# Four short attention runs for the first two head groups, and VectorE in ScalarE's place in the preparation of token blocks

## The chip, the cores and the metric

The kernel runs on one core of a Trainium2 chip. The metric is the device time of one execution, in microseconds. Four compute engines matter: TensorE (PE) multiplies matrices, ScalarE (ACT) evaluates functions such as the exponential, VectorE (DVE) and GpSimd (POOL) do elementwise work, and SyncE (SP) issues most of the transfers. Each runs its own instructions strictly in order and waits for the others by semaphores.

## The reference

One transformer block with adaptive layer norm, on 2048 tokens of width 512 and 32 heads of width 16:

```python
x = A_x
mod = (_silu(c) @ w_mod).reshape(c.shape[0], 6, 1, -1)
sa, ca, ga, sb, cb, gb = (mod[:, 0], ..., mod[:, 5])
h = _layernorm(x) * (1 + ca) + sa
x = x + ga * _A_ref(h, A_wqkv, A_wo)      # softmax(q k^T / 4) v, 32 heads, then wo
h = _layernorm(x) * (1 + cb) + sb
x = x + gb * _B_ref(h, B_w1, B_b1, B_w2, B_b2)   # w1 (512 x 1376), gelu, w2
```

## The kernel before

**Tiles and runs.** Tokens are cut into four blocks of 512 (`b` = 0 to 3) and sixteen key tiles of 128 (`kt`). The heads are cut into four column groups of eight (`cc`), each into two halves of four heads (`par`). One *run* is the attention of four heads for one block of 512 queries over a list of key tiles; the four heads of a run share the rows of TensorE. A *unit* is the score tile of one head and one key tile, 128 keys by 512 queries. A run over all sixteen tiles has 64 units, and the whole kernel has 2048 units' worth of scores.

**Who takes the exponential.** Most units go to ScalarE: TensorE writes three or two units into a PSUM tile `st` (`qk_a`, matmuls recorded at `qk`'s lines 940 and 944), and one ACTIVATE at line 998 turns them into `pt`. The two sizes alternate, 128x1536 and 128x1024, with one `st` tile each and four `pt` buffers each. The tiles in `shared` (key tiles 2, 5, 8, 11 and 14, `DKS`) go to VectorE where it gets to them first: it adds a constant to the scores (line 1052, `ph`), so that the integer, read as bf16, approximates the exponential, and makes shifted copies (`ph` at line 1087, `sh` at line 1096, and GpSimd pieces at line 1103), which are multiplied by v and by a weighted v (`VWB`). The products with v are accumulated in one PSUM tile `od` (line 1147), which VectorE copies out when a run ends (`normalise`, line 1214). Denominators then go through transfers on SP's queue (`dn`, `dc`, `rn`, `RB`), and GpSimd multiplies by the reciprocals.

**The start.** Before k, q and v of a token block exist, its 512 tokens have to be loaded, normalised (VectorE: line 660 and 661 statistics, line 676 normalisation, with the root on GpSimd, line 671), transposed by TensorE, modulated by (1 + ca) and sa into `blk` (`modulate`, line 686 on ScalarE or line 689 on VectorE), multiplied by the weights (`make_k`, `make_v`, `make_q`), and cast from PSUM to `kT` (line 694 on ScalarE or line 696 on VectorE) and to `VEB` (line 696). To begin early, the first two runs (`SUB = 2`: the two halves of group 0 for query block 0) read only key tiles 0 to 3, that is the first token block, and leave their partial sums in SBUF (`kept`). Runs 2 and 3 are the same two halves over key tiles 4 to 15, and `normalise` adds the kept sums (line 1211). From run 4 on all sixteen tiles are read. Blocks 1 and 2 (`PARTS`) are modulated and cast in two parts of 256 tokens, the first part's modulations on VectorE and the second part's on ScalarE; blocks 0 and 3 in whole rows. In this text the second and third token blocks are `b` = 1 and 2 in the code.

**The order.** The kernel writes its own instruction order. A planner (`Plan`) in the program keeps a list of ready operations for each engine, with assumed durations, and issues the one with the best priority (`dyn`); VectorE's units of a run may begin only when ScalarE has reached that run (`d_job` and the main loop's test against `a_run`). A small pseudo-random term (`spread`) is added to the priorities, seeded by one entry of `SEEDS` for each 12.5 us of planned time. So the table `SEEDS` picks one order out of many. Nothing is decided at run time.

Of the kernel before, what the change touches and what calls it, by code (L numbers as in the profile page):

```python
# [11 lines left out]
ACT = mybir.ActivationFunctionType  # L12
# [43 lines left out]
AL = 0.06  # L56
FILL = 1.6
SPREAD = 0.3
SEEDS = (47, 74, 926, 0, 261, 311, 918, 742, 253, 869, 717, 310, 0, 77, 989, 722, 609, 0, 307, 361, 371, 367, 117, 577, 633, 569, 261, 103, 97, 26, 695, 543, 331, 469, 527, 375, 85, 71, 0, 418, 210, 266, 573, 349, 750, 566, 887, 0, 37, 0, 351, 423, 527, 370, 279, 111, 267, 2, 850, 0, 0, 0, 0, 0, 0, 0)
HEAT = 1.45  # L60
RISK = 0.2

# [207 lines left out]
def kernel(  # L270
# [19 lines left out]
    NC = D // P  # L290
    NT = S // P
    QB = 512
    NQ = S // QB
    LAST = NQ - 1
    TPB = QB // P
# [49 lines left out]
    PARTS = (1, 2)  # L345
# [269 lines left out]
    def silu(o):  # L615
# [8 lines left out]
              prio=0.0, rel=(o_tr,))  # L624
# [167 lines left out]
    def make_k(b, cc, kind, acq, eng, after=None):  # L792
        if b in PARTS and cc == 0:
            o_k[(cc, b)] = []
            for part in range(2):
                cols = slice(2 * part * P, 2 * (part + 1) * P)
                mm = chain([(lambda ps, j=j, cols=cols: nc.tensor.matmul(
                    out=ps[:, 0:2 * P], lhsT=o_w[1].tile[:, j, 0:P], rhs=o_h[b].tile[:, j, cols],
                    start=(j == 0), stop=(j == NC - 1)), MM / 2) for j in range(NC)], [o_w[1], o_w0[1]], kind, acq,
                    (o_h[b], o_w[1]), need=lambda j, part=part: o_hd[b][NC * part + j])  # L800
                o_k[(cc, b)].append(op(eng, lambda o, mm=mm, cols=cols: copy(eng, kT[cc][b][:, cols], mm.tile[:, 0:2 * P]),
                                       0.33, (mm,), prio=0.3, rel=(mm,)))
            return
        if b == cc == 0:
            turns, mm, o_k[(cc, b)] = (0, 2, 1, 3), None, []
            for e, lo in (("ACT", 0), ("DVE", 2 * P)):
                cols = slice(lo, lo + 2 * P)
                mm = chain([(lambda ps, n=n, j=j, cols=cols: nc.tensor.matmul(
                    out=ps[:, 0:2 * P], lhsT=o_w[1].tile[:, j, 0:P], rhs=o_h[0].tile[:, j, cols],
                    start=(n == 0), stop=(n == NC - 1)), MM / 2) for n, j in enumerate(turns)], [o_w[1], o_w0[1], mm], kind, acq,  # L810
                    (o_h[0], o_w[1]), need=lambda n: o_hd[0][turns[n]])
                o_k[(cc, b)].append(op(e, lambda o, e=e, mm=mm, cols=cols: copy(e, kT[0][0][:, cols], mm.tile[:, 0:2 * P]),
                                       0.27 if e == "ACT" else 0.33, (mm,), prio=0.01 if e == "ACT" else 0.2, rel=(mm,)))
            return
        mm = proj(b, o_w[1], cc, kind, acq, after)
        o_k[(cc, b)] = op(eng, lambda o: copy(eng, kT[cc][b], mm.tile[:, 0:QB]), 0.6 if eng == 'DVE' else 0.5, (mm,), prio=0.3,
                          rel=(mm,))
# [54 lines left out]

    early = [(1, 0),(0, 1),(1, 1)]
    groups = [(0, 0)] + early + [(b, cc) for b in range(NQ) for cc in range(NC) if (b, cc) not in [(0, 0)] + early]
    SUB = 2
    runs = [(0, p) for p in range(SUB)] + [(b, 2 * cc + p) for b, cc in groups[:LAST * NC] for p in range(2)] + [(LAST, u) for u in range(6)] + [(LAST, 6), (LAST, 7)] * 2
    wait = {cc: 2 * groups.index((0, cc)) for cc in range(NC)}
    NR = len(runs)
    HB = QB // 2
# [8 lines left out]


    def tiles_of(r):  # L890
        return range(len(PAIRS)) if r in part_of else range(TPB) if r < SUB else range(TPB if r < 2 * SUB else 0, NT)
    shared = [[0, 1] if r in part_of else [kt for kt in (() if r < SUB else FIRST_DKS if r == SUB else DKS)
                                           if kt in tiles_of(r)] for r in range(NR)]
    own = [[kt for kt in tiles_of(r) if kt not in shared[r]] for r in range(NR)]
# [52 lines left out]
                         qm.tile[rows, :, hb * HB:(hb + 1) * HB], start=True, stop=True)  # L947

    def qk_deps(r, kt):
        n = r if r < SUB else r - SUB  # L950
        want_q(n // 2 + 1 + (n >= LAST * 8 - 4) if n < LAST * 8 - 2 else n - LAST * 4 + 3)
        cc, par, hb = run_heads(r)
        qm, evs = o_q[(cc, runs[r][0])]
        got = [evs[par or 0]]
        for t in key_tiles(r, kt):
            k = o_k[(cc, t // TPB)]
            got.append(k[t % TPB // 2] if isinstance(k, list) else k)
        return got, qm
# [243 lines left out]
        o_mv[n] = dma(shift, (ml,), kb=32, n=5.4, prio=0.5)  # L1202
    o_mv = [None, None]

    kept = []

    def normalise(r):
        last, od = o_last[r], o_od[r]
        if r in range(SUB, 2 * SUB):
            OD = kept[r - SUB]  # L1210
            got = op("DVE", lambda o: nc.vector.tensor_tensor(out=OD.tile, in0=od.tile, in1=OD.tile, op=ALU.add), 0.6,
                     (last, OD), lat=0.3, prio=0.0, rel=(od,))
        else:
            got = OD = op("DVE", lambda o: nc.vector.tensor_copy(out=o.tile, in_=od.tile), 0.6, (last,), lat=0.3,  # L1214
                          prio=0.0, acq=r_OD, rel=(od,))
        if r < SUB:
            kept.append(OD)
            return
        st = {}

        def d1(o):
            st["dn"] = drp.tile([4, QB], FP32, name="dn")
            nc.sync.dma_start(out=st["dn"], in_=OD.tile[16:P:32, :])
        o1 = dma(d1, (got,), kb=8, n=1.4, prio=0.0)
        o2 = dma(lambda o: nc.sync.dma_start(
            out=o.tile, in_=st["dn"].rearrange("i (s e) -> (i s) e", e=16)), (o1,), kb=8, n=1.4, prio=0.0,
            acq=r_dc)
# [24 lines left out]
        def shift(o):  # L1252
            for i in range(4):
                nc.sync.dma_start(out=to.tile[32 * i + 16:32 * i + 32, 0:HB] if b == LAST else
                                  to.tile[32 * i + 16:32 * i + 32, :],
                                  in_=OT.tile[32 * i:32 * i + 16, HB:QB] if b == LAST else
                                  OT.tile[32 * i:32 * i + 16, :])
        mv = dma(shift, two + ([] if b == LAST else to.two), kb=64, n=5.4, prio=0.5,
                 rel=() if b == LAST else (OT,))
        to.two = [mv]  # L1260
        if b == LAST:
            o_OT[(b, u)] = OT
# [326 lines left out]
    for b in range(NQ):  # L1589
        kind = f"in{b}"  # L1590
        urgent.add(kind)
        o_h[b], o_hd[b], za, trs = layer_norm(
            lambda t, b=b: o_x[b].tile[:, t, :], o_x0 if b == 0 else [o_x[b]] * TPB, modA, o_mA, prev_tr, r_blk,
            ("DVE", "ACT") if b in PARTS else ("DVE", "DVE", "ACT", "ACT") if b < 3 else ("DVE",) * 4, tuple(r_st[::-1]) if b == 0 else (r_ax, r_ax), kind, 0.6 + 0.2 * b, after, by_part=b in PARTS)
        prev_tr = trs[-1]
        if b == 0:
            op("NIL", first_done, 0.0, za, lat=0.0, prio=0.0)
        o_h[b].uses += 1
        free(o_x[b], za)
        if b == 0:  # L1600
            make_q(0, 0, kind, None)
        after = [za[-1]] * TPB if b else [o_hd[0][2]] * 1 + [o_q[(0, 0)][1][0]] * 3
        make_k(b, 0, kind, r_ax, "ACT")
        make_v(b, 0, kind, r_ax, "DVE", None if b else o_k[(0, 0)][0])
    o_w[0].uses += 1
    for cc in range(1, NC):
# [26 lines left out]
    while True:  # L1633
# [7 lines left out]
        while ended:  # L1641
            r = ended.pop(0)
# [90 lines left out]
```

## Time and profile before

| | us |
|---|---|
| median of 3 runs | 752.58 |
| lowest, highest | 752.27, 754.48 |
| the profiled execution | 752.77 |
| its span in the trace | 751.0 |
| granted TensorE clock, share of full speed | 0.997 |

The span runs from the first to the last instruction; the execution's own time has some 1.8 us around it. In a list of groups each row gives the line, the engine, the operation, output and inputs with partitions x elements, and the count; behind the bar come the busy time in us and the mean duration in ns, and behind the second bar the time the engine sat idle in front of these instructions and what ended it. In a timeline each row gives the start in us, the duration of the merged rows together, the engine and line, and in brackets an idle time in front of it. Instructions of one engine overlap in these records: one starts before the one ahead has drained, so the distance between two starts, not the sum of durations, tells what an instruction costs a full queue. Line numbers of the kernel before are used; in the changed kernel, lines from about 890 on are one to three higher.

A few groups that the later sections use, as the page lists them:

| group | count | busy us | mean ns |
|---|---|---|---|
| L1103 GpSimd, pieces of the shifted copy | 487 | 216.2 | 463 |
| L1087 VectorE, `ph` copy | 132 | 90.9 | 689 |
| L1096 VectorE, `sh` copy | 132 | 128.0 | 972 |
| L660 VectorE, statistics | 32 | 21.7 | 678 |
| L1214 VectorE, copy of `od` | 30 | 20.5 | 683 |

### The profile page before, as it was taken

Reading aid. Unit: us, or ns where it says so; the run is one execution under the profiler, and the core shown is the slowest. Engines: PE = TensorE matmul, PEld = TensorE weight load, DVE = VectorE, ACT = ScalarE, POOL = GpSimd, SP = SyncE. Lnnn points to the kernel's source line nnn. Section 1 sums busy time; section 2 is a strip of 40 time slices with the busy share of each in tenths; the row PEclk is TensorE's granted clock in tenths of the full one; section 3 lists DMA queues with packets and bytes.
Section 4 is the critical chain, followed back from the end, with each engine's and each line's share of the span. In section 5 each row is a group of like instructions: output and inputs, shape, how many; then the busy total and the mean of one; then the engine's idle time right before and its main releaser. Section 6 shows DMA issues by size and latency. Waiting matters only on the chain.

```text
span 751.0 us, 20442 instructions
## 1 busy us (share of the span) xinstructions
PE 700.1 (93%) x8287; PEld 262.9 (35%) x8358; DVE 693.7 (92%) x1179; ACT 729.8 (97%) x659; POOL 325.5 (43%) x743
## 2 busy tenths in 40 slices
PE   8898999999999999999999999999999999999897
PEld 4433333233323223233223332322244343434564
DVE  6988999899999999999999999999899999997983
ACT  4999999999999999999999999999999999999995
POOL 5223534555434444555556434354343543343420
PEclk9999999999999999999999999999999999999999
DMA  7024001000011110000100100000111000110100
GB/s 224 30 93 147 24 20 47 23 10 22 16 27 45 51 48 24 10 27 13 45 19 23 31 23 20 27 23 26 32 50 30 18 19 18 46 26 20 54 5 29
DMA packets 38712, 27.93 MB, mean 37 GB/s; under 512 B 17793, under 2 KB 34146, under 8 KB 38618
## 3 DMA queue, kind: packets, MB, share of 16 engines
q1 hardware_dynamic: 38610, 26.62, 12.3%
q8 instruction: 65, 1.06, 0.6%
q14 instruction: 29, 0.24, 0.1%
q10 hardware_dynamic: 8, 0.00, 0.0%
HBM read 21.03 MB, written 2.59 MB: 31 GB/s over the span
## 4 chain that ended last, share of the span: by engine, by line
ACT 75%; PE 15%; DVE 6%; issue 3%; DVEq 0%; POOL 0%; POOLq 0%
ACT pt L998 73%; PE od L1147 4%; PE st L944 3%; DVE ph L1052 3%; PE ax L1363 1%; PE ax L1420 1%; DVE sh L1096 1%; DVE ph L1087 1%; PE t L1363 1%; PE ax L944 1%; PE od L1135 1%; PE st L940 1%; ACT g L1436 1%; PE od L480 1%; ACT blk L686 0%
## 5 line engine op out<-in xcount | busy, mean ns | idle before, releaser
L998 ACT ACTIVATE pt<-st 128x1536 bf16<-128x1536 f32 x608 | 689.8, 1358 | 2.6 <-PE st L944 1.5
L1052 DVE TENSOR_SCALAR ph<-ax 128x512 int16<-128x512 f32 x528 | 345.9, 684 | 28.5 <-PE ax L944 20.5
L1103 POOL TENSOR_TENSOR sh<-ph,step 128x128 int32<-128x128 int32 x487 | 216.2, 463 | 300.4 <-DVE ph L1087 110.3
L944 PE MATMUL st<-qm,kT 32*128 32x512 bf16 x1416 | 222.0, 383 | 23.3 <-ACT pt L998 18.7
L944 PE MATMUL ax<-qm,kT 32*128 32x512 bf16 x504 | 166.8, 380 | 2.3 <-DVE ph L1052 1.4
L944 PEld LDWEIGHTS <-kT 32*128 32x128 bf16 x1920 | 72.4, 91 | 219.0 <-issue 208.9
L1147 PE MATMUL od<-pt,VEB 128*32 128x512 bf16 (+1 forms) x1696 | 131.6, 348 | 1.1 <-DVE OD L1214 0.6
L1096 DVE TENSOR_SCALAR sh<-ph 128x2816 int16<-128x2816 int16 (+4 forms) x132 | 128.0, 972 | 1.0
L1147 PEld LDWEIGHTS <-VEB 128*32 128x32 bf16 x2912 | 67.5, 95 | 100.6 <-issue 85.3
L1147 PE MATMUL od<-sh,VWB 128*32 128x512 bf16 (+1 forms) x1216 | 94.1, 348 | 4.3 <-DVE sh L1096 4.0
L1147 PE MATMUL od<-ph,VEB 128*32 128x512 bf16 (+1 forms) x1216 | 94.7, 348 | 2.2 <-DVE ph L1087 1.3
L1087 DVE TENSOR_SCALAR ph<-ph 128x2048 int16<-128x2048 int16 x132 | 90.9, 689 | 1.0
L1147 PEld LDWEIGHTS <-VWB 128*32 128x32 bf16 x1216 | 32.3, 95 | 45.4 <-issue 39.1
L1244 POOL TENSOR_TENSOR OT<-OD,RB 128x128 bf16<-128x128 f32 x72 | 32.0, 459 | 27.5 <-DVE sh L1096 19.8
L1420 PE MATMUL ax<-blk,W 128*128 128x512 bf16 (+1 forms) x156 | 41.1, 351 | 1.5 <-issue 0.3
L1244 POOL TENSOR_TENSOR OS<-OD,RB 128x128 bf16<-128x128 f32 x48 | 21.3, 457 | 24.9 <-DVE sh L1096 18.9
L786 PE MATMUL ax<-blk,w 128*128 128x512 bf16 x88 | 29.6, 382 | 2.5 <-issue 1.0
L1363 PE MATMUL ax<-w,g 128*128 128x512 bf16 x85 | 25.1, 382 | 1.6 <-DVE ph L1052 0.8
L1424 DVE TENSOR_SCALAR g<-ax,b1c 128x512 bf16<-128x512 f32 x33 | 24.5, 745 | 0.8 <-PE ax L1420 0.7
L660 DVE BATCH_NORM_STATS2 ln_s<-xb 128x6 f32<-128x512 bf16 x32 | 21.7, 678 | 1.6 <-DMA xb<-in_A_x_dram 1.5
L1214 DVE COPY OD<-od 128x512 f32<-128x512 f32 x30 | 20.5, 683 | 1.0 <-PE od L1147 0.9
L1420 PEld LDWEIGHTS <-W 128*128 128x128 bf16 x176 | 14.2, 97 | 20.2 <-issue 13.0
(144 smaller groups left out, 473.8 us busy)
## 6 DMA issues: line engine op xcount, KB each, us to landing
RB<-rn SPq DMA_DIRECT2D x120, 64.0 KB
xb<-in_A_x_dram SPq DMA_DIRECT2D x8, 512.0 KB
out_dram<-o SPq DMA_DIRECT2D x16, 128.0 KB
qm<-qs SPq DMA_DIRECT2D x120, 16.0 KB
W<-in_B_w_dram SPq DMA_DIRECT2D x1, 1376.0 KB
w<-in_A_wqkv_dram SPq DMA_DIRECT2D x3, 384.0 KB
blk<-in_w_mod_dram SPq DMA_DIRECT2D x2, 512.0 KB
xb<-in_w_mod_dram SPq DMA_DIRECT2D x2, 512.0 KB
```

The lines of the kernel that those rows point to most:

```text
L786: return chain([(lambda ps, j=j, n=n: nc.tensor.matmul(out=ps[:, 0:QB], lhsT=w.tile[:, j, cc * P:(cc + 1) * P], rhs=o_h[b].tile[:, j, :], ...
L944: nc.tensor.matmul(out=o.tile[:, k * QB:(k + 1) * QB], lhsT=kT[cc][kb][rows, ko * P:(ko + 1) * P], rhs=qm.tile[rows, par, :] if hb is None ...
L998: exps.append(nc.scalar.activation(out=e.tile[:, 0:len(got) * QB], in_=o.tile[:, 0:len(got) * QB], func=ACT.Exp, scale=ESC))
L1052: nc.vector.tensor_scalar(out=ph.tile[:, c0:c0 + QB], in0=o.tile, scalar1=PH_B, scalar2=-PH_SH[1], op0=ALU.add, op1=ALU.max)
L1087: a = in_turn(op("DVE", lambda o: nc.vector.tensor_scalar(out=first.tile[:, n:2 * n], in0=first.tile[:, 0:n], scalar1=PH_SH[1], scalar2=No ...
L1096: b = in_turn(op("DVE", lambda o: nc.vector.tensor_scalar(out=into.tile[:, 0:cols], in0=first.tile[:, 0:cols], scalar1=PH_SH[2], scalar2=None,
L1103: after_dve(nc.gpsimd.tensor_tensor(out=into.tile[:, at:at + w].bitcast(I32), in0=first.tile[:, at - n:at - n + w].bitcast(I32), in1=step, ...
L1147: nc.tensor.matmul(out=o_od[r].tile[32 * i:32 * i + 32, n * HB:n * HB + w], lhsT=(VWB[:, DKS.index(kt), c0:c0 + 32] if weighted else v_til ...
L1244: two = beside(lambda c: nc.gpsimd.tensor_tensor(out=OT.tile[:, c], in0=OD.tile[:, c], in1=o5.tile[:, c], op=ALU.mult), (OT,), (OD, o5))
L1363: nc.tensor.matmul(out=ps, lhsT=g[:, f, col:col + P], rhs=rhs, start=(f == 0), stop=(f == NF - 1))
L1420: mm = chain([(lambda ps, f=f, j=j: nc.tensor.matmul(out=ps[:, 0:N], lhsT=W1[:, j, f * P:(f + 1) * P], rhs=h.tile[:, j, 0:N], start=(j == ...
L1424: ev.append(op("DVE", lambda o, f=f, mm=mm: nc.vector.tensor_scalar(out=g.tile[0:last(f), f, 0:N], in0=mm.tile[0:last(f), 0:N], scalar1=b1 ...
```

## The change

The first two head halves, which were attended in two short runs (tiles 0 to 3) and two long ones (tiles 4 to 15), are now attended in four short runs (tiles 0 to 3 for both, then tiles 4 to 7 for both) and two of eight tiles (8 to 15). Partial sums are kept after the first two runs and added to after the next two, and again at the end. VectorE's units may begin in the fifth run instead of the third. For the second and third token block VectorE modulates both parts, and VectorE casts k of the second, third and fourth block; ScalarE keeps half of the modulation and of the cast of the first block only. `SEEDS` is another table, with all entries up to the last ones new.

```diff
-SEEDS = (47, 74, 926, 0, 261, 311, 918, 742, 253, 869, 717, 310, ...
+SEEDS = (665, 903, 0, 563, 966, 382, 0, 419, 805, 807, 343, 983, ...
...
-    SUB = 2
-    runs = [(0, p) for p in range(SUB)] + [...]
+    SUB = 4
+    runs = [(0, p % 2) for p in range(SUB)] + [...]
...
     def tiles_of(r):
-        return range(len(PAIRS)) if r in part_of else range(TPB) if r < SUB else range(TPB if r < 2 * SUB else 0, NT)
+        return range(len(PAIRS)) if r in part_of else range(r // 2 * TPB, r // 2 * TPB + TPB) if r < SUB else range(
+            SUB // 2 * TPB if r < SUB + 2 else 0, NT)
...
     def qk_deps(r, kt):
-        n = r if r < SUB else r - SUB
+        n = r % 2 if r < SUB else r - SUB
...
-    kept = []
+    kept, kept_at = [], [None, None]
 
     def normalise(r):
         last, od = o_last[r], o_od[r]
-        if r in range(SUB, 2 * SUB):
-            OD = kept[r - SUB]
+        if 2 <= r < SUB + 2:
+            OD = kept[r % 2]
             got = op("DVE", lambda o: nc.vector.tensor_tensor(out=OD.tile, in0=od.tile, in1=OD.tile, op=ALU.add), 0.6,
-                     (last, OD), lat=0.3, prio=0.0, rel=(od,))
+                     (last, kept_at[r % 2]), lat=0.3, prio=0.0, rel=(od,))
         else:
             got = OD = op("DVE", lambda o: nc.vector.tensor_copy(out=o.tile, in_=od.tile), 0.6, (last,), lat=0.3,
                           prio=0.0, acq=r_OD, rel=(od,))
+        if r < 2:
+            kept.append(OD)
         if r < SUB:
-            kept.append(OD)
+            kept_at[r % 2] = got
             return
...
-            ("DVE", "ACT") if b in PARTS else ("DVE", "DVE", "ACT", "ACT") if b < 3 else ("DVE",) * 4, ...
+            ("DVE", "DVE") if b in PARTS else ("DVE", "DVE", "ACT", "ACT") if b < 3 else ("DVE",) * 4, ...
...
-        make_k(b, 0, kind, r_ax, "ACT")
+        make_k(b, 0, kind, r_ax, "ACT" if b == 0 else "DVE")
```

More of the change, by code (lines that the diff above doesn't have):

```diff
@@ L58 @@
 SPREAD = 0.3
-SEEDS = (47, 74, 926, 0, 261, 311, 918, 742, 253, 869, 717, 310, 0, 77, 989, 722, 609, 0, 307, 361, 371, 367, 117, 577, 633, 569, 261, 103, 97, 26, 695, 543, 331, 469, 527, 375, 85, 71, 0, 418, 210, 266, 573, 349, 750, 566, 887, 0, 37, 0, 351, 423, 527, 370, 279, 111, 267, 2, 850, 0, 0, 0, 0, 0, 0, 0)
+SEEDS = (665, 903, 0, 563, 966, 382, 0, 419, 805, 807, 343, 983, 0, 269, 0, 791, 325, 327, 357, 625, 0, 930, 83, 837, 414, 921, 261, 859, 495, 283, 463, 819, 202, 377, 258, 914, 431, 854, 874, 147, 126, 965, 658, 601, 119, 149, 683, 681, 0, 933, 902, 0, 217, 45, 113, 0, 465, 189, 475, 0, 0, 0, 0, 0, 0, 0)
 HEAT = 1.45
@@ L874 @@
     groups = [(0, 0)] + early + [(b, cc) for b in range(NQ) for cc in range(NC) if (b, cc) not in [(0, 0)] + early]
-    SUB = 2
-    runs = [(0, p) for p in range(SUB)] + [(b, 2 * cc + p) for b, cc in groups[:LAST * NC] for p in range(2)] + [(LAST, u) for u in range(6)] + [(LAST, 6), (LAST, 7)] * 2
+    SUB = 4
+    runs = [(0, p % 2) for p in range(SUB)] + [(b, 2 * cc + p) for b, cc in groups[:LAST * NC] for p in range(2)] + [(LAST, u) for u in range(6)] + [(LAST, 6), (LAST, 7)] * 2
     wait = {cc: 2 * groups.index((0, cc)) for cc in range(NC)}
@@ L1593 @@
             lambda t, b=b: o_x[b].tile[:, t, :], o_x0 if b == 0 else [o_x[b]] * TPB, modA, o_mA, prev_tr, r_blk,
-            ("DVE", "ACT") if b in PARTS else ("DVE", "DVE", "ACT", "ACT") if b < 3 else ("DVE",) * 4, tuple(r_st[::-1]) if b == 0 else (r_ax, r_ax), kind, 0.6 + 0.2 * b, after, by_part=b in PARTS)
+            ("DVE", "DVE") if b in PARTS else ("DVE", "DVE", "ACT", "ACT") if b < 3 else ("DVE",) * 4, tuple(r_st[::-1]) if b == 0 else (r_ax, r_ax), kind, 0.6 + 0.2 * b, after, by_part=b in PARTS)
         prev_tr = trs[-1]
```

## The prediction

> **What bounds the kernel now.** I read the busy shares first, then the chain of work that ended last, then ScalarE's groups.
>
> ```profile
> span 751.0 us, 20442 instructions
> PE 700.1 (93%) x8287; PEld 262.9 (35%) x8358; DVE 693.7 (92%) x1179; ACT 729.8 (97%) x659; POOL 325.5 (43%) x743
> ...
> ACT 75%; PE 15%; DVE 6%; issue 3%; DVEq 0%; POOL 0%; POOLq 0%
> ...
> L998 ACT ACTIVATE pt<-st 128x1536 bf16<-128x1536 f32 x608 | 689.8, 1358 | 2.6 <-PE st L944 1.5
> L1052 DVE TENSOR_SCALAR ph<-ax 128x512 int16<-128x512 f32 x528 | 345.9, 684 | 28.5 <-PE ax L944 20.5
> ```
>
> Three engines are above 90%, but only ScalarE (ACT) is on the chain for most of the span, and 689.8 us of it is one group, the exponentials. They take three or two score units of 128x512 in turn, so 608 of them are 1520 units; VectorE (DVE) makes the other 528 units with its integer route. ScalarE waited 2.6 us in all in front of them. VectorE waited 28.5 us in front of its own units, so it has a little room. In the stretches between front and tail:
>
> ```profile
> 13.90:43.00 29.10, 24.34 (x241) 12.00 (x240) 26.62 (x67) 29.10 (x34) 6.56 (x15) 1.00 0.22 69
> 43.00:731.00 688.00, 647.78 (x7798) 236.18 (x7857) 651.28 (x1074) 686.01 (x596) 309.08 (x699) 1.00 0.12 33
> ```
>
> The columns are PE, weight loads, VectorE, ScalarE, GpSimd, then the granted clock. ScalarE is busy for 29.10 of 29.10 us while the later token blocks are still being prepared, so whatever it does there besides exponentials moves the end. That work shows in ScalarE's timeline:
>
> ```profile
> 13.84 8.23 ACT L998 ACTIVATE pt<-st 128x1536 bf16<-128x1536 f32 x7 [0.76 <-PE st L944]
> 21.89 1.99 ACT L686 ACTIVATE blk<-ax,modA 128x256 bf16<-128x256 bf16 x4
> 23.69 0.45 ACT L694 CAST kT<-ax 128x256 bf16<-128x256 f32 x1
> 23.94 1.12 ACT L998 ACTIVATE pt<-st 128x1024 bf16<-128x1024 f32 x1
> 24.86 0.47 ACT L694 CAST kT<-ax 128x256 bf16<-128x256 f32 x1
> 25.11 4.74 ACT L998 ACTIVATE pt<-st 128x1536 bf16<-128x1536 f32 x4
> 29.59 2.08 ACT L686 ACTIVATE blk<-ax,modA 128x256 bf16<-128x256 bf16 x4
> 31.39 0.55 ACT L694 CAST kT<-ax 128x256 bf16<-128x256 f32 x1
> 31.64 2.56 ACT L998 ACTIVATE pt<-st 128x1536 bf16<-128x1536 f32 x2
> 33.88 0.58 ACT L694 CAST kT<-ax 128x256 bf16<-128x256 f32 x1
> 34.14 8.44 ACT L998 ACTIVATE pt<-st 128x1536 bf16<-128x1536 f32 x7
> 42.54 0.59 ACT L694 CAST kT<-ax 128x512 bf16<-128x512 f32 x1
> 43.02 28.15 ACT L998 ACTIVATE pt<-st 128x1024 bf16<-128x1024 f32 x25
> ```
>
> Instructions of one engine overlap here (a cast of 0.45 us starts 0.25 us ahead of the next row), so I price by the distance between starts, not by the durations. From 13.84 to 21.89, with nothing missing, seven exponentials (18 units) take 8.05 us: **0.447 us a unit**. Over the whole kernel a unit takes 689.8 / 1520 = 0.454 us.
>
> **The change part by part.** I counted each engine's instructions in both programs.
>
> *Taken off ScalarE.* Eight modulations: 23.69 - 21.89 = 1.80 and 31.39 - 29.59 = 1.80, so 3.60 us. Five casts of k: 0.25 (23.69 to 23.94), 0.25, 0.25, 0.26 and 0.48 (42.54 to 43.02), so 1.49 us. Together **-5.09 us**, all on the path.
>
> The Trainium skill speaks against moving them: "VectorE: DVE Perf Modes", Specifications, has ScalarE closer to PSUM and VectorE closer to SBUF, and all thirteen read PSUM. The trace bears that out for the casts alone (0.48 on ScalarE for 512 columns, 0.60 for such a pass on VectorE below), not for the modulations (0.45 against 0.32); by the rule the move would lose only if VectorE were the last to end, which is priced below.
>
> *Put on ScalarE.* The changed program has 305 exponentials of 1536, 304 of 1024 and one of 512: 1524 units, four more, since VectorE now begins its units later and makes 524. 4 x 0.454 = **+1.82 us**. Bounds: 4 x 0.447 = 1.79, and four separate 512-wide exponentials at the 0.48 of the wide cast, 1.92.
>
> *Put on VectorE.* It gets the modulations and casts and two more additions of partial sums (the two extra runs); it loses four units, one 128x2048 and one shift pass. Its own rows from the stretch in question:
>
> ```profile
> 13.93 0.41 DVE L696 CAST kT<-ax 128x256 bf16<-128x256 f32 x1
> 14.75 0.69 DVE L660 BATCH_NORM_STATS2 ln_s<-xb 128x6 f32<-128x512 bf16 x1 [0.41 <-DMA xb<-in_A_x_dram]
> ...
> 15.58 0.66 DVE L660 BATCH_NORM_STATS2 ln_s<-xb 128x6 f32<-128x512 bf16 x1
> ...
> 16.37 0.66 DVE L696 CAST VEB<-ax 128x512 bf16<-128x512 f32 x1
> 16.95 0.28 DVE L863 TENSOR_SCALAR VWB<-ax 128x128 bf16<-128x128 f32 x1
> 17.14 0.69 DVE L660 BATCH_NORM_STATS2 ln_s<-xb 128x6 f32<-128x512 bf16 x1
> ...
> 20.20 0.74 DVE L676 TENSOR_SCALAR z<-xb,mv,rs 128x512 bf16<-128x512 bf16 x2 [0.28 <-POOL rs L671]
> 20.85 1.36 DVE L689 TENSOR_SCALAR blk<-ax,modA 128x256 bf16<-128x256 bf16 x4
> 22.13 0.68 DVE L660 BATCH_NORM_STATS2 ln_s<-xb 128x6 f32<-128x512 bf16 x1
> ...
> 34.18 0.68 DVE L1214 COPY OD<-od 128x512 f32<-128x512 f32 x1
> 34.78 0.29 DVE L863 TENSOR_SCALAR VWB<-ax 128x128 bf16<-128x128 f32 x1
> ...
> 38.89 1.90 DVE L689 TENSOR_SCALAR blk<-ax,modA 128x512 bf16<-128x512 bf16 x4 [0.47 <-PE ax L742]
> 40.71 0.68 DVE L1052 TENSOR_SCALAR ph<-ax 128x512 int16<-128x512 f32 x1
> ```
>
> A modulation is 0.32 (four from 20.85 to 22.13), a 512-wide pass 0.60 (34.18 to 34.78). Work that costs ScalarE 5.09 us costs VectorE at most 8 x 0.32 + 4 x 0.41 + 0.60 = 4.8, and it gives up 4 x 0.684 of units. So its load hardly changes, and averaged over the span this hides in its idle time. What is left to ask is whether it is in time with the **k of the last block**, tokens 1536 to 2047, whose cast it now makes.
>
> The order on VectorE from the row at 13.93 up to that cast: five casts of k (0.41), twelve statistics pairs (0.80, from 14.75 to 16.37 by two), three casts of v (0.58), four weighted v (0.19), twelve normalisations (0.65 for two), sixteen modulations of 256 (0.32) and four of 512 (0.455), and seven 512-wide passes (0.60: two copies and two additions of partial sums, one q, two score units): 2.05 + 9.60 + 1.74 + 0.76 + 3.90 + 5.12 + 1.82 + 4.20 = 29.2 us. With the 0.41 of the DMA wait the cast starts at 43.5; with another 1.0 of waits for GpSimd as before it is 44.5:
>
> ```profile
> DVE z L676 <- POOL rs L671: 1.0, 3, 0.3
> ```
>
> The cast takes 0.6, and some 0.7 later an exponential can run (below): 44.8 to 45.8. ScalarE first needs that k in its 29th exponential, 70 units in: 13.84 + 70 x 0.447 = 45.1. One of the additions ahead of the cast (the fourth run's) waits for unit 64 to be exponentiated (mean 1.36) and multiplied by v (some 0.5), 13.84 + 64 x 0.447 + 1.9 = 44.4; with the addition, a score unit and the cast behind it (1.8), k would be there at 46.2 and the exponential at 46.9. So ScalarE stands here between 0 and 1.8 us; I take 0.6, near the middle of the first pair. The stretch before already holds a stand: from 13.84 to 43.02 it made 53 units (23.70) and the 5.09 above, 28.79 of 29.18, so 0.39. Net **+0.2 us** (-0.4 to +1.4).
>
> ```profile
> 12.71 0.37 ACT L694 CAST kT<-ax 128x256 bf16<-128x256 f32 x1 [0.99 <-PE ax L808]
> ...
> 13.40 0.39 PE L944 MATMUL st<-qm,kT 32*128 32x512 bf16 x3
> ```
>
> The 0.7 is 0.32 from that cast's end (13.08) to the score group that reads it, and 0.44 from there to the exponential at 13.84.
>
> *Other moves.* Two more run ends mean two more hand-overs of the one accumulator, each a 0.60 pass that stops the multiplication by v, not the scores; eight `pt` buffers, about 8.9 us of exponentials, cover that. On SP's queue the denominators of the sixth run (second group, tokens 1024 on) now stand ahead of the reciprocals of the fifth, so the latter are held until the sixth run ends; who waits is the next copy of a partial sum two runs on, 64 units or about 29 us later. The large weight loads keep their place behind the first denominators. I cost these at nothing.
>
> *The order searched anew.* This has no row. How well an order feeds ScalarE shows as the stretch of the 1520 units over the undisturbed rate: 689.8 - 1520 x 0.447 = 10.0 us. The room before it is TensorE's:
>
> ```profile
> PE st L944 <- ACT pt L998: 18.7, 55, 0.8
> ...
> 744.94 1.89 PE L1363 MATMUL t<-w,g 128*128 128x512 bf16 x8
> 746.67 0.81 PE L1363 MATMUL t<-W2c,g 128*128 128x512 bf16 x3
> ```
>
> TensorE waited 18.7 us for score banks; where it didn't, ScalarE may have stood. A 512-column matmul takes 1.73 / 8 = 0.216 us. Adding the matmuls between one score group and the next at that price, two gaps in a row exceed the two exponentials they must hide under by over 0.5 us at 60 places before and 54 after; mode changes between scores, values and full matmuls fall from 1250 to 1224. So the new order is about as dense as the old: I take **0**, with bounds of -5 (the stretch halved) and +5 (half as much again).
>
> **Sum.** Against its own time, 752.77 us (span 751.0 and 1.8 around it): 752.77 - 5.09 + 1.82 + 0.2 = **749.7 us**. That run lies 0.2 above the median of 752.58, so I write 749.6.
>
> The Trainium skill prices the moved work by itself: "ScalarE: Activation LUTs", What ACT_TABLE_LOAD costs, gives 186 ns and 0.833 a column, 93 for each pointer operand, less 93 of overlap. An estimate by that page is 0.49 for a modulation, where the trace has 0.45, and the sum would come out 0.3 us lower; the trace's figure stands.
>
> **The rivals.**
> 1. *The order eats the gain.* The stretch grows by about 3 us: 752.6, no change. For it: 18.7 us of room over 610 score groups is 0.03 us each, and every place of the order is new. Against it: the counts above.
> 2. *The last k is late.* VectorE stands behind the addition as worked out, 1.8 instead of 0.6: 750.8, no change by measurement. For it: the queue is full, 26.62 of 29.10 before. Against it: only one place, and the next order can catch nothing up.
> 3. *TensorE's order falls behind: slower.* Overlong gaps between score groups in the new order use up the 18.7 us of room, so that the stretch grows from 10 to 18 us: 757.6. It decides from the point where the added stretch exceeds 754.8 - 749.6 = 5.2 us. For it: half of the old stretch again is nearly enough, and ScalarE's own wait of 2.6 shows how exactly the old order was fitted. Against it: TensorE's work and mode changes don't grow.
> 4. *ScalarE's share isn't freed:* the four added units become more, which the counts exclude; no chance.
>
> **How the numbers follow.** About 0.3% (2.3 us) is what a measurement of this kernel can tell from no change: faster is below 750.3, slower above 754.8. The forecast, with orders that are better, has 0.50; rival 1 has 0.19, rival 2 has 0.14, rival 3 has 0.17. Faster 0.50, same 0.33, slower 0.17. The forecast's own range is 746.8 to 750.3; with rivals 1 and 2 and the nearer half of rival 3 the range is 746.8 to 755.2.
>
> **What would show it.** Right: no modulation of 256 and no cast of k on ScalarE behind the first exponential; exponentials back to back from 13.84 to about 45; 1524 units in some 691 to 692 us; the table load behind the last exponential 3 us earlier, and the 18.8 us from it to the end unchanged:
>
> ```profile
> 732.21 1.28 ACT L1429 ACT_TABLE_LOAD   x1
> ```
>
> Rival 2 shows as a ScalarE wait around 45 us in front of the exponential that first reads the last block's k. Rivals 1 and 3 show as a stretch above 13 or 15 us, with TensorE's wait for score banks well under 18.7. I am wrong if the first exponential moves, if the clock in the first 45 us falls below 1.00, or if VectorE's wait in front of its units falls while ScalarE's grows.

## The result, and the profile after

The changed kernel takes 749.11 us (median of 14 runs, 748.46 to 752.2) against 752.35 for the kernel before (14 runs on the same chips). The ratio is 0.996, with a 95% interval of 0.9948 to 0.9972: faster by 0.4%, where 749.6 was forecast. The profiled execution took 748.80. (One run of e12 below, 801.62 us at a mean clock of 0.970, fell in a slower state of the chip and is left out of its median and ratio.)

The page of the changed kernel, with the lines that answer to those of before:

```profile
span 747.0 us, 20473 instructions
...
PE 696.9 (93%) x8307; PEld 262.9 (35%) x8376; DVE 693.7 (93%) x1188; ACT 726.8 (97%) x648; POOL 322.6 (43%) x734
...
ACT 71%; PE 16%; DVE 9%; issue 3%; DMA 1%; POOL 0%; DVEq 0%
...
L999 ACT ACTIVATE pt<-st 128x1536 bf16<-128x1536 f32 x610 | 690.8, 1360 | 2.2 <-PE ax L945 0.9
L1053 DVE TENSOR_SCALAR ph<-ax 128x512 int16<-128x512 f32 x524 | 342.2, 682 | 22.1 <-PE ax L945 14.8
```

ScalarE is still the bound. It has two exponentials more and eleven instructions fewer in all. VectorE's busy time is the same 693.7 us, since what it took over and what it gave up are alike. Its idle time in front of its units went from 28.5 to 22.1 us.

ScalarE's timeline and the two stretches (columns as in the prediction):

```profile
13.70 31.75 ACT L999 ACTIVATE pt<-st 128x1536 bf16<-128x1536 f32 x28 [0.76 <-PE st L945]
46.38 29.49 ACT L999 ACTIVATE pt<-st 128x1536 bf16<-128x1536 f32 x26 [0.94 <-PE ax L945]
...
728.44 1.28 ACT L1432 ACT_TABLE_LOAD   x1
```

```profile
13.90:43.00 29.10, 24.62 (x248) 11.76 (x247) 26.72 (x71) 29.10 (x27) 6.40 (x14) 1.00 0.33 107
43.00:728.00 685.00, 645.08 (x7814) 236.53 (x7882) 651.46 (x1078) 683.42 (x594) 306.44 (x691) 1.00 0.11 31
```

From 13.70 on, 28 exponentials (70 units) stand back to back where thirteen other instructions stood before; then ScalarE is idle for 0.94 us, in front of the exponential that reads k of the last block for the first time. The table load behind the last exponential comes at 728.44 instead of 732.21.

The 4.0 us between the two spans can be followed by the distances between ScalarE's starts (a 1536-wide exponential holds the next one back by 1.331 us, a 1024-wide one by 0.904 when nothing is missing):

| step | us |
|---|---|
| first exponential earlier, 13.84 to 13.70 | -0.14 |
| thirteen instructions gone | -5.08 |
| four units more | +1.81 |
| standing at the last block's k: 0.39 before, 1.28 now (idle and delay) | +0.89 |
| all other delays behind exponentials: 10.96 before, 9.70 now | -1.26 |
| tail behind the table load, 18.79 to 18.56 | -0.23 |
| sum | -4.01 |

The saving in the other delays has one main place. The windows of TensorE around 130 us, before:

```profile
128.40:131.85 3.45, 2.44 (x38) 1.38 (x36) 3.03 (x4) 3.45 (x4) 1.15 (x3) 1.00 0.19 57
131.85:135.26 3.41, 3.41 (x29) 0.62 (x28) 1.74 (x5) 2.81 (x3) 2.13 (x6) 0.50 0.11 29
```

In the second window the granted clock (third column from the right) was 0.50 for 3.41 us, and ScalarE stood twice in it or just behind it:

```profile
133.91 1.02 ACT L998 ACTIVATE pt<-st 128x1024 bf16<-128x1024 f32 x1 [0.27 <-PE ax L944]
135.44 3.72 ACT L998 ACTIVATE pt<-st 128x1536 bf16<-128x1536 f32 x3 [0.50 <-PE st L944]
```

The two exponentials behind these waits started late by 0.57 and 0.62 us in distances of starts, 1.2 together. The changed kernel has no such window between its first exponential and its last. So 1.2 of the 4.0 us of this pair of profiles hangs on one clock window of the kernel before. Runs sorted by their mean granted clock bear this out in part:

| mean granted clock | before, us | changed, us |
|---|---|---|
| 1.00 | 751.08 to 751.87 (5 runs) | 748.46 to 749.21 (9 runs) |
| 0.997 or 0.998 | 751.93 to 752.59 (10) | 749.73 to 750.16 (3) |
| 0.990 to 0.993 | 754.52 to 754.95 (5) | 751.78, 752.2 |

(The 22 runs of before are those of the first experiments; two of them, 751.53 at 0.999 and 752.64 at 0.995, are in no row.) At a clock of 1.00 the medians are 751.80 and 748.98: 2.8 us, which is the 4.0 less the 1.2. But between the second and the first row of the kernel before lie only 0.5 us by medians (752.30 and 751.80).

### The profile page after: what moved, and what is told of

Read it like the earlier page. It is cut to its first block, busy times and chain, and to the rows that moved or that the text cites. A ratio compares the mean times of both kernels' runs of the same rounds, so it can differ in the third digit from the quotient of the medians.

```text
span 747.0 us, 20473 instructions
## 1 busy us (share of the span) xinstructions
PE 696.9 (93%) x8307; PEld 262.9 (35%) x8376; DVE 693.7 (93%) x1188; ACT 726.8 (97%) x648; POOL 322.6 (43%) x734
## 4 chain that ended last, share of the span: by engine, by line
ACT 71%; PE 16%; DVE 9%; issue 3%; DMA 1%; POOL 0%; DVEq 0%
ACT pt L999 70%; DVE ph L1053 4%; PE od L1148 3%; PE st L945 3%; PE t L1366 1%; PE ax L1423 1%; DVE sh L1097 1%; PE st L941 1%; PE od L1136 1%; PE ax L945 1%; DVE ph L1088 1%; PE ax L1366 1%; ACT g L1439 1%; PE ax L786 1%; PE ax L1360 1%
## 5 line engine op out<-in xcount | busy, mean ns | idle before, releaser
L1053 DVE TENSOR_SCALAR ph<-ax 128x512 int16<-128x512 f32 x524 | 342.2, 682 | 22.1 <-PE ax L945 14.8
L1104 POOL TENSOR_TENSOR sh<-ph,step 128x128 int32<-128x128 int32 x478 | 214.0, 468 | 299.8 <-DVE sh L1097 123.6
L945 PE MATMUL st<-qm,kT 32*128 32x512 bf16 x1424 | 222.9, 383 | 25.5 <-ACT pt L999 20.2
L945 PE MATMUL ax<-qm,kT 32*128 32x512 bf16 x496 | 163.6, 379 | 4.0 <-DVE ph L1053 3.0
L1148 PE MATMUL od<-ph,VEB 128*32 128x512 bf16 (+1 forms) x1192 | 91.9, 347 | 2.5 <-DVE ph L1088 1.4
L1148 PE MATMUL od<-sh,VWB 128*32 128x512 bf16 (+1 forms) x1192 | 92.3, 347 | 1.7 <-DVE sh L1097 1.2
L1088 DVE TENSOR_SCALAR ph<-ph 128x2048 int16<-128x2048 int16 x131 | 88.9, 681 | 0.8
L1148 PEld LDWEIGHTS <-VWB 128*32 128x32 bf16 x1192 | 30.5, 95 | 39.7 <-issue 33.8
L1247 POOL TENSOR_TENSOR OS<-OD,RB 128x128 bf16<-128x128 f32 x48 | 22.8, 487 | 22.4 <-DVE ph L1088 10.9
L786 PE MATMUL ax<-blk,w 128*128 128x512 bf16 x91 | 29.2, 382 | 1.8 <-DVE ph L1053 0.7
```

The source lines that it names most:

```text
L786: return chain([(lambda ps, j=j, n=n: nc.tensor.matmul(out=ps[:, 0:QB], lhsT=w.tile[:, j, cc * P:(cc + 1) * P], rhs=o_h[b].tile[:, j, :], ...
L945: nc.tensor.matmul(out=o.tile[:, k * QB:(k + 1) * QB], lhsT=kT[cc][kb][rows, ko * P:(ko + 1) * P], rhs=qm.tile[rows, par, :] if hb is None ...
L1053: nc.vector.tensor_scalar(out=ph.tile[:, c0:c0 + QB], in0=o.tile, scalar1=PH_B, scalar2=-PH_SH[1], op0=ALU.add, op1=ALU.max)
L1088: a = in_turn(op("DVE", lambda o: nc.vector.tensor_scalar(out=first.tile[:, n:2 * n], in0=first.tile[:, 0:n], scalar1=PH_SH[1], scalar2=No ...
L1104: after_dve(nc.gpsimd.tensor_tensor(out=into.tile[:, at:at + w].bitcast(I32), in0=first.tile[:, at - n:at - n + w].bitcast(I32), in1=step, ...
L1148: nc.tensor.matmul(out=o_od[r].tile[32 * i:32 * i + 32, n * HB:n * HB + w], lhsT=(VWB[:, DKS.index(kt), c0:c0 + 32] if weighted else v_til ...
```

## The experiments

Twelve kernels were run. In the first four and in e9 to e11 the planned order is kept instruction by instruction, and only the engine or the place of a few instructions changes. Beside the time I read how long after the first exponential the 22nd, the 29th and the 41st start (53, 70 and 100 units), which shows the first stretch without what comes later. Each ratio is to the kernel before as it ran beside that experiment.

| run | median us | ratio to before (95%) | 53 units | 70 units | 100 units |
|---|---|---|---|---|---|
| before | 752.35 | | 29.2 | 36.8 | 50.2 |
| changed | 749.11 | 0.996 (0.9948 to 0.9972) | 23.7 | 32.7 | 46.1 |
| e1 all thirteen on ScalarE | 757.21 | 1.0049 (1.0029 to 1.0069) | 29.9 | 40.1 | 53.5 |
| e2 eight modulations on ScalarE | 755.62 | 1.0047 (1.0028 to 1.0066) | 28.9 | 39.7 | 53.1 |
| e3 order of before, thirteen on VectorE | 757.29 | 1.0067 (1.0047 to 1.0087) | 32.5 | 41.0 | 54.4 |
| e4 last normalisation ahead | 749.70 | 0.9965 (0.9951 to 0.9979) | 23.7 | 32.7 | 46.1 |
| e5 plain order of before | 789.59 | 1.0483 (1.0446 to 1.052) | 29.9 | 41.2 | 54.6 |
| e6 plain order, VectorE moves alone | 786.72 | 1.0467 (1.0423 to 1.0512) | 23.7 | 40.3 | 54.0 |
| e7 plain order, four short runs alone | 785.51 | 1.043 (1.041 to 1.045) | 29.3 | 36.9 | 51.4 |
| e8 plain order, both | 789.72 | 1.0485 (1.0444 to 1.0526) | 23.7 | 32.9 | 46.3 |
| e9 as e1, TensorE kept busier | 756.86 | 1.0057 (1.0039 to 1.0075) | 28.6 | 39.7 | 53.3 |
| e10 as e2, TensorE kept busier | 755.07 | 1.0031 (1.0014 to 1.0049) | 28.8 | 38.4 | 52.0 |
| e11 as e3, TensorE kept busier | 757.12 | 1.0061 (1.004 to 1.0081) | 31.8 | 41.0 | 54.4 |
| e12 changed, seed table of before | 790.32 | 1.0524 (1.0461 to 1.0587) | | | |

### The thirteen back on ScalarE: e1, e2, e9, e10

```diff
-                        e, h.tile[:, j, cols], one.ps[:, j, :], mod, j),
+                        "ACT" if part else e, h.tile[:, j, cols], one.ps[:, j, :], mod, j),
...
-    copy(eng, kT[cc][b][:, cols], mm.tile[:, 0:2 * P])
+    copy("ACT", kT[cc][b][:, cols], mm.tile[:, 0:2 * P])
```

(e2 has only the first edit.)

> The changed kernel with its planned order kept instruction by instruction, but the eight modulations and five casts of k issued on ScalarE again, at the same places of the order. My theory (the gain is the ScalarE time of these thirteen, 5.09 us by the distances of starts, less four more units): ScalarE gets 5.1 us back, and the 0.9 us it stands at the last block's k goes, since VectorE is freed of some 4.5 us of work ahead of that cast: +4.2 us on the changed kernel's 749.1, 753.3 (752.5 to 754.3), so slower than the kernel before, by the 1.8 us of the four units less what the new order saves. Rival (the gain is the new order's, and ScalarE had room for the thirteen): at most +2, 751.1 or below.

> As the run before, but only the eight modulations go back to ScalarE; the casts stay on VectorE. My theory: +3.6 us for the modulations, -0.9 for the stand at the last k, which goes as VectorE is freed of 2.6 us ahead of it: +2.7, 751.8 (751.0 to 752.8). If instead the casts carry the gain (each may hold ScalarE longer than the distance of starts shows), it stays below 750.2. The difference to the run before prices the casts: 1.5 by my theory.

Both lost more than expected, by 3.9 and 3.8 us, so the rival that ScalarE had room for the thirteen falls, and so does the one that the casts alone carry the gain (e1 lies 1.6 above e2). Windows of e1:

```profile
22.90:26.32 3.42, 2.10 (x23) 0.77 (x20) 2.47 (x7) 3.42 (x7) 0.99 (x3) 1.00 0.42 143
26.32:33.15 6.83, 6.42 (x40) 2.65 (x38) 2.96 (x8) 5.84 (x8) 0.86 (x2) 0.50 0.01 4
```

With ScalarE slower, TensorE had less to do (2.10 of 3.42 us; 2.80 in the changed kernel in the same window), and the clock was then halved for 6.83 us, and again from 43.4 on. So e9 and e10 repeat them with idle matmuls:

```diff
-            if o.extra:
+            if o.extra or left[r] > 0 and (r < SUB or r == SUB and left[r] % 2):
                 zeros(r)
```

> The first run again (changed order, all thirteen on ScalarE), with 17 groups of four idle matmuls of 512 columns (0.22 us each, multiplied by a zero weight, so that nothing is added) behind products with v of the first five runs. In the first run TensorE's granted clock was halved from 26.3 to 33.2 and from 43.4 to 50.2, and the 100th unit came 53.5 us after the first exponential (46.1 in the changed kernel). My theory now: the thirteen cost ScalarE 5.1 us, and the rest of the loss is the halved clock, which came because TensorE waited more. With the clock held at 1.00 in the first 60 us the 100th unit comes after 50.3 to 51.3 us, time 753.3 to 754.5. Rival (the rest is the order: TensorE's and VectorE's queues were fitted to a ScalarE without the thirteen): 52.5 us or more, 756 to 758, though the clock is held.

> The second run again (only the eight modulations on ScalarE), with the same idle matmuls. There the 100th unit came after 53.1 us. My theory: 46.1 + 3.6 for the modulations, less up to 0.9 of the stand at the last k: 48.8 to 49.8 us, time 751.8 to 752.9, and 1.5 below the run with all thirteen. Rival (order, not clock): 52 us or more, 755.

The first halving went; one from about 41 us on stayed in both (6.83 us in e9, 3.41 in e10). So the condition of both theories, a clock held at 1.00, wasn't met, and the 53.3 and 52.0 us for 100 units and the medians lie where the rivals had them. Three runs of e10 kept a mean clock of 1.00: 753.19, 753.29 and 753.30, which is 4.3 above the changed kernel at that clock (748.98) and nearer the theory (751.8 to 752.9) than the rival (755). The eight modulations explain 3.6 of it; no trace shows where the other 0.7 lies. In e9 the first 53 units, nearly all of them ahead of the late halving, took 28.6 us against 23.7: 4.9 more, where the eight modulations and the four narrow casts ahead of that point were priced at 4.6. In e10 they took 28.8, which is 5.1 more for 3.6 of modulations; the rest are delays, 0.87 of them at 43.11, inside the halving. By distances of starts the twelve take 4.60 us in e9 and the eight 3.59 in e10. So what the thirteen cost ScalarE is as priced. What I had wrong is the rest: I expected the stand at the last k to go, but it stayed (0.93 us at 52.69 in e10, 0.94 in the changed kernel), and others came. ScalarE, and one row of TensorE, in e10:

```profile
43.11 1.02 ACT L999 ACTIVATE pt<-st 128x1024 bf16<-128x1024 f32 x1 [0.73 <-PE st L945]
44.65 7.10 ACT L999 ACTIVATE pt<-st 128x1536 bf16<-128x1536 f32 x6 [0.52 <-PE st L945]
52.69 3.71 ACT L999 ACTIVATE pt<-st 128x1536 bf16<-128x1536 f32 x3 [0.93 <-PE ax L945]
```

```profile
41.09 1.01 PE L797 MATMUL ax<-blk,w 128*128 128x256 bf16 x4 [2.01 <-ACT blk L686]
```

TensorE waits 2.01 us for ScalarE's modulations of the third block, since ScalarE comes to them later than in the changed kernel VectorE did; e1, e2 and e9 hold the same wait, of 2.00 or 2.01 us, at 40.7 to 42.1. The next scores stand behind it on TensorE in an order that was fitted to a ScalarE without the thirteen, and the halved clock begins within 1.3 us of its end. How much of ScalarE's delays is the order and how much the halved clock of the same microseconds isn't separated. The difference of e9 and e10, the casts, is 1.8 us by medians (1.5 expected); part of it may be the clock, since no run of e9 had a mean clock of 1.00.

### The moves without the four short runs: e3, e11

The same edits with "DVE" in the kernel before.

> The kernel before, its planned order kept instruction by instruction, with the thirteen issued on VectorE: the moves without the four short runs. My theory: ScalarE is freed of 5.1 us, but VectorE, busy 26.6 of 29.1 us there and already making units of the third run, gets some 4.5 us more and is late with k of the second to fourth block, so that ScalarE stands 2 to 4 us in the first 45 us where it stood 0.4: 749.8 to 752.0, with waits of ScalarE for scores of the third and fourth block. Rival (the short runs are not needed, VectorE has the room): 752.4 - 5.1 = 747.3, with no such waits. Second rival (VectorE stays behind to the end): above 752.4.

> The third run again (the order of before with two short runs, all thirteen on VectorE), with the same idle matmuls. There ScalarE stood 3.7 us at 23.2 us, ahead of the first halved window at 27.3, and the 100th unit came after 54.4 us, against 50.2 in the kernel before. My theory: the first stand is k of the second block coming late from VectorE, and only part of the rest is the clock: 51 to 53.5 us, time 754 to 756.5, still slower than before. Rival (all of it is the clock): 46 to 48 us and 748 to 750, so the short runs were not needed.

ScalarE's and TensorE's timelines of e3:

```profile
28.23 2.55 ACT L998 ACTIVATE pt<-st 128x1024 bf16<-128x1024 f32 x2 [3.46 <-PE st L944]
...
38.31 2.37 ACT L998 ACTIVATE pt<-st 128x1536 bf16<-128x1536 f32 x2 [2.90 <-PE st L944]
```

```profile
25.57 0.61 PE L797 MATMUL ax<-blk,w 128*128 128x256 bf16 x4 [1.75 <-DVE blk L689]
26.49 1.15 PE L847 MATMUL ax<-w,blk 128*128 128x128 bf16 x16 [0.31 <-DVE kT L696]
27.58 0.60 PE L944 MATMUL st<-qm,kT 32*128 32x512 bf16 x2
```

ScalarE is freed of 5.1 us and loses more. VectorE is late, as I expected, but not where I expected it. The stand of 3.46 us is in front of the 10th exponential, with 23 units done, and the first two runs hold 32 units: it still reads k of the first block. Its scores (27.58) stand on TensorE behind the products for k and v of the second block, and these wait 1.75 and 0.31 us for VectorE's modulations and cast. The 15th exponential, which stands 2.90 us, reads k of the second block, cast by 28.4, behind the third block's products. So what ScalarE waits for is TensorE's fixed order, into which the moved instructions come late, and not yet the deadline of a k. The idle matmuls change nothing: in e11 the first stand (4.06 us) begins before any halving, and TensorE waits 1.67 and 1.43 us for modulations of the second and third block. The loss was larger than the 2 to 4 us I gave it. The rival that the short runs aren't needed falls for this order. The time is in the range of the second rival, that VectorE stays behind to the end, but the 100th unit is already 4.2 us later than in the kernel before, so nearly all of the loss comes ahead of it. What an order searched for the moves with two short runs would give wasn't tried.

### The stand at the last k: e4

```diff
-            copy(eng, dst[:, :, :, 0:16], mm.tile[:, 0:QB].rearrange(...))
+            later_on(b, cc, lambda: copy(eng, dst[:, :, :, 0:16], src))
...
+        if len(applied) == NT:
+            for fn in held:
+                fn()
```

`later_on` holds back the third block's cast of v and the weighted v until the last normalisation has been issued.

> The changed kernel in its planned order, but on VectorE the last normalisation of the last block stands ahead of the cast of v and the two weighted v of the third block, which in the trace delay it by 0.99 us (38.68 to 39.67). My theory (the stand at the last k is a chain of VectorE's queue: last normalisation, transposes, modulations, product, cast): the chain moves 0.5 to 1.0 us ahead and ScalarE's 0.94 us of idle shrinks to 0.0 to 0.4, time 748.2 to 748.7 against 749.1. Rival (the chain is held by TensorE, since the second pair of transposes waits for a bank that a score unit of VectorE holds until 42.3): the stand stays at 0.7 or more, time 749.0.

The rival was right: no gain (at a mean clock of 1.00 the medians are 748.95 in e4 and 748.98 in the changed kernel). In e4 the four normalisations stand together at 38.24, a microsecond ahead of where the last one was, but the modulations behind them start no earlier against the first exponential:

```profile
38.24 1.37 DVE L676 TENSOR_SCALAR z<-xb,mv,rs 128x512 bf16<-128x512 bf16 x4
...
41.35 0.99 DVE L700 TENSOR_SCALAR blk<-ax,modA 128x512 bf16<-128x512 bf16 x2 [0.74 <-PE ax L753]
...
45.74 0.69 DVE L707 CAST kT<-ax 128x512 bf16<-128x512 f32 x1
```

This run's first exponential is 0.53 later (14.23), and so are the modulations (41.35 against 40.82) and the cast (45.74 against 45.22). What holds the chain, as far as the trace of the changed kernel shows, is TensorE's order and what VectorE has ahead of the cast; no run moved these:

```profile
40.82 0.99 DVE L689 TENSOR_SCALAR blk<-ax,modA 128x512 bf16<-128x512 bf16 x2 [0.74 <-PE ax L742]
42.30 0.69 DVE L1053 TENSOR_SCALAR ph<-ax 128x512 int16<-128x512 f32 x1 [0.48 <-PE ax L945]
43.08 0.99 DVE L689 TENSOR_SCALAR blk<-ax,modA 128x512 bf16<-128x512 bf16 x2
44.01 0.69 DVE L1212 TENSOR_TENSOR OD<-od,OD 128x512 f32<-128x512 f32 x1
44.62 0.68 DVE L1053 TENSOR_SCALAR ph<-ax 128x512 int16<-128x512 f32 x1
45.22 0.69 DVE L696 CAST kT<-ax 128x512 bf16<-128x512 f32 x1
```

```profile
42.65 0.40 PE L742 MATMUL ax<-ident,z 128*128 128x128 bf16 x4
...
43.56 0.40 PE L1148 MATMUL od<-pt,VEB 128*32 128x512 bf16 x4
...
45.44 0.91 PE L945 MATMUL st<-qm,kT 32*128 32x512 bf16 x5
```

The last four transposes stand at 42.65 on TensorE, behind scores for VectorE and for ScalarE, though their input has been there since 40.1. Then the addition of the partial sum (44.01), which needs the product at 43.56, and a score unit (44.62) stand ahead of the cast.

### The parts in unsearched orders: e5 to e8

```diff
-SEEDS = (665, 903, 0, 563, ...)
+SEEDS = (0,) * 66
```

> The kernel before with all entries of the seed table zero: the planner's plain order, not searched. Its program has 1560 units on ScalarE instead of 1520. My theory (a unit more on ScalarE costs what a unit costs there, 0.454 us): 752.3 + 40 x 0.454 = 770.5 (768 to 773). Rival (the planner's own order feeds the engines worse beyond the count): above 775.

> As the plain order of before, with the thirteen instructions planned and issued on VectorE, but two short runs: 1560 units on ScalarE as well. My theory: 5.1 us less on ScalarE, given back in part by 2 to 4 us of waits for k of the second to fourth block: 2 to 3 us below the plain order of before, 768 (766 to 770). Rival (short runs are not needed where the planner knows of the move): 5 us below it, 765.5.

> The changed kernel with a zero seed table and the thirteen instructions on ScalarE as before: the four short runs alone, unsearched. 1552 units on ScalarE. My theory: the runs by themselves free nothing on ScalarE, so the time follows the units: 752.3 + 32 x 0.454 = 766.8, 3.6 us below the plain order of before (2 to 5). Rival (the shorter runs cost more hand-overs of the accumulator than they save): no better than the plain order of before.

> The changed kernel with a zero seed table: both parts, unsearched. 1552 units on ScalarE. My theory: the runs alone less 5.1 us of ScalarE's work plus about 1 us of standing at the last block's k: 4 us below the run before, 762.8 (761.5 to 764.5), and 7 to 8 us below the plain order of before. Rival (the gain of the change is that of its search): within 2 us of the runs alone, and the two plain orders differ by less than 4 us.

The times missed: the four medians lie between 785 and 790, some 19 to 27 us above what I gave; for e5 the rival's range is right. e6 and e7 came out 2.9 and 4.1 below e5 (2 to 3 and 3.6 expected), in a scatter of up to 7 us between the runs of one kernel, but e8, with both parts, 4.2 above e7 and level with e5. That is what the rival of e8 says of the two plain orders: as a whole the change gains no time there without a seed table searched for it. Where the rest went shows in e5 in the tail, for one:

```profile
779.49 0.81 ACT L686 ACTIVATE blk<-t,modB 128x128 bf16<-128x128 bf16 x2 [11.70 <-PE t L1539]
```

ScalarE waits 11.7 us for the last tile, where it waited 1.4 before; and the delays between exponentials, 11 us before, add up to 20 to 31 us in the four. e8 has the most: 29.9 us of them behind the 100th unit, against 18.8 in e5, so it loses there what it gained. For it does gain: the first 100 units take 54.6 us with neither part, 54.0 with the moves alone, 51.4 with the short runs alone and **46.3 with both**, as in the searched changed kernel (46.1). The moves bring 5.1 us with the short runs and 0.6 without; the short runs bring 3.2 alone. In e5 and e7, though, the clock was halved once within these units (36.28 to 39.70 and 50.84 to 54.25), in e6 and e8 it wasn't. If the delays of 1.18 and 1.09 us that stand there are put down to that, the moves bring 4.0 us with the short runs and lose 0.6 without. In e6 ScalarE's wait for k of the last block shows why, in one row, beside the same place in e8:

```profile
47.51 3.71 ACT L998 ACTIVATE pt<-st 128x1536 bf16<-128x1536 f32 x3 [8.63 <-PE st L944]
```

```profile
46.67 10.49 ACT L999 ACTIVATE pt<-st 128x1536 bf16<-128x1536 f32 x9 [1.15 <-PE ax L945]
```

With two short runs the last k is needed after 55 units (its cast starts at 46.27), with four after 70.

### The other seed table: e12

```diff
-SEEDS = (665, 903, 0, 563, ...)
+SEEDS = (47, 74, 926, 0, ...)
```

> The changed kernel with the seed table of before: both parts, in an order that was searched for another program. 1556 units on ScalarE instead of 1524. By the units alone: 749.1 + 32 x 0.454 = 763.6. But the four plain orders came out some 20 us above their units, in stands after the first 100 units and a longer tail, so my theory now is that a table that wasn't searched for the program is worth no more than none: 778 to 792, with the first 100 units nevertheless after 46 to 47 us. Rival (the old table still fits in large part): 763 to 768.

The ratio of 1.0524 is that of no table at all (1.043 to 1.0485) or worse, so the theory held for the time. What it says of the first 100 units isn't tested: in the profiled execution the clock was halved from 17.60 to 34.67 us.

## Why the prediction was right, point by point

**The bound.** Right: ScalarE's queue from the first exponential to the last sets the end, 3.6 of the 4.0 us lie between them and the table load, and nothing else moved by more than 0.3. The first exponential, whose moving was to be a sign against the prediction, came 0.14 earlier; it lies between 13.58 and 14.28 us in the kernels here.

**Taken off ScalarE, -5.09.** Right: 5.08 in the trace, confirmed from the other side by e9 (4.9 more for 4.6 priced, 4.60 by distances of starts). The rule cited from the Trainium skill ("VectorE: DVE Perf Modes", Specifications), that ScalarE is closer to PSUM, would have spoken against it only with VectorE as the last to end, and VectorE's busy time came out unchanged.

**Four units, +1.82.** Right: 1.81.

**VectorE in time, net +0.2 (-0.4 to +1.4).** The mechanism was right, at its place: an idle ScalarE at 45.4 in front of the exponential that reads the last k. The size was off: 1.28 of delay instead of 0.6, net +0.89. The step mis-sized is the choice of 0.6 from the first pair, 44.8 to 45.8 (against 45.1 that is -0.3 to 0.7, so 0.6 is its late end and not near its middle); the working for the addition ahead of the cast (exponential at 46.9) came nearer, since the cast started at 45.22 behind just that addition and a score unit, and the exponential at 46.38. That is rival 2, which did happen, at 0.7 of the 1.2 us it was given beyond the forecast, and was more than covered by the next term.

**The new order, 0 (-5 to +5).** The other delays fell by 1.26, as much as the halved clock window that the kernel before had at 131.85 explains (1.2). So the orders are as dense as one another, as the counts of matmuls between score groups had it, and the prediction had no term for the clock. (The 10.0 us that it gave the old stretch above the undisturbed rate is 10.4 with the figures as written, and 11.3 by distances of starts.) TensorE's wait for score banks went from 18.7 to 20.2:

```profile
PE st L945 <- ACT pt L999: 20.2, 60, 0.6
```

Rivals 1 and 3 needed this to shrink; it grew, and all delays of ScalarE together went from 11.3 to 11.0 us.

**The sum.** The terms added up to -3.07 us; the profiled pair differs by 4.0, and runs at a clock of 1.00 by 2.8. In the pair the 0.69 missed at the last k was outweighed by 1.26 of other delays and 0.37 of an earlier start and a shorter tail, none of which was forecast. That the time came out 0.5 below the forecast and not above it is luck, and so is part of the nearness.

**Other moves at nothing.** Nothing in the trace speaks against it; they weren't tried one by one.

**What the prediction couldn't tell** is that its two parts depend on one another. It weighed the moves against ScalarE's time and used the short runs only for the deadline of the last k; e6 shows that without that deadline moved the moves gain next to nothing, and e3 and e11 that they lose in an order that wasn't planned for them. Nor could it tell that the gain in time needs the seed table as well: e8 and e12 have both parts and no gain.

## What to carry to other kernels

Price an instruction on a full engine by the distance between starts, not by its duration: 0.45 and 0.25 us here, where the rows said 0.68 and 0.49. Before moving work to another engine, ask by when its result is needed there, and move the deadline first: in the plain orders the moves bring 4 to 5 us of the first 100 units with the short runs and next to nothing without. The time of a change in an order that was searched as a whole can't be judged in an order that wasn't (33 to 41 us off here); measure the stretch that it touches, and search again before you read the time.

## What the runs showed of the hardware

In these traces TensorE's granted clock is halved for 3.41 us (the kernel before) or a multiple of it: 6.83 in e1, 10.24 in e3, 17.07 in e12. The Trainium skill, "TensorE: Matmul & The Clock Gate", Part 1, gives a window of 3413 ns, which agrees. The Trainium skill, "TensorE: Matmul & The Clock Gate", HAM oscillation, asks for no idle gaps above about 3.4 us. Here a halving came without one: ahead of the first in e1 the longest single wait was 0.90 us:

```profile
24.71 0.39 PE L945 MATMUL st<-qm,kT 32*128 32x512 bf16 x3 [0.90 <-ACT pt L999]
```

TensorE's busy share ahead of a halving doesn't sort the cases either. It was 2.44 of 3.45 us in the kernel before and 2.10 of 3.42 in e1. But the changed kernel kept its clock behind a window with 2.38 of 3.41 (the first line), and e1 lost it behind one with 3.26 of 3.41 (the second and third):

```profile
21.56:24.97 3.41, 2.38 (x29) 1.11 (x28) 3.28 (x10) 3.41 (x5) 0.92 (x2) 1.00 0.47 154
```

```profile
128.72:132.13 3.41, 3.26 (x32) 0.94 (x31) 3.41 (x6) 3.41 (x4) 1.04 (x3) 1.00 0.13 27
132.13:135.54 3.41, 3.41 (x31) 0.76 (x30) 2.26 (x7) 2.50 (x3) 0.45 (x1) 0.50 0.31 87
```

So what decides stays open. By the runs' times the difference between a mean clock of 0.997 or 0.998 and one of 1.00, about one halved window, is between 0.5 and 2.4 us in these kernels (752.30 against 751.80 by medians for the kernel before, 749.7 to 750.2 against 748.98 for the changed kernel, 754.9 to 755.7 against 753.3 for e10), and it comes in some executions of a kernel and not in others.
